# Transposing normalised tokens and attention output by DMA, with the settings of the order of work chosen anew

## Chip, cores and metric

The kernel runs on one core of one Trainium2 chip. The metric is the time of one execution on the device in microseconds (us). A core has five engines with lists of instructions of their own: TensorE (PE, with its weight loads PEld), VectorE (DVE), ScalarE (ACT), GpSimd (POOL) and SyncE (SP), which here issues all DMAs.

## The reference

Two layers of attention and feed-forward on 2048 tokens of width 512, in bfloat16; attention has 32 heads of 16 channels, the feed-forward part 1792 channels. Both layers use the same weights.

```
def _A_ref(x, wqkv, wo):                        # H = 32, Dh = 16
    q, k, v = split((x @ wqkv).reshape(B, S, 3, H, Dh))
    p = softmax(einsum("bhqd,bhkd->bhqk", q, k) * Dh ** -0.5)
    return einsum("bhqk,bhkd->bhqd", p, v).reshape(B, S, D) @ wo
def _B_ref(x, w_gate, w_up, w_down):
    return (gelu(x @ w_gate) * (x @ w_up)) @ w_down
x = A_x
x = x + _A_ref(_layernorm(x), A_wqkv, A_wo)
x = x + _B_ref(_layernorm(x), B_w_gate, B_w_up, B_w_down)
x = x + _A_ref(_layernorm(x), A_wqkv, A_wo)
x = x + _B_ref(_layernorm(x), B_w_gate, B_w_up, B_w_down)
```

## The kernel before

**Attention.** Tokens are cut into blocks of queries: four of 512 in layer 0, three of 512 and two of 256 in layer 1, the last of these split into two halves of 128 for its last two groups. A *unit* is one block and one group of four heads. Each unit passes twice over the scores. In pass 1 TensorE makes score tiles of 128 queries x 512 keys (line 2236) into PSUM banks 0 to 3, and DVE takes the maximum of each row (`p1_emit`, line 2251), for two banks in one instruction where two are free (128x1024), else for one (128x512). A *folded* tile is another way to these maxima: TensorE makes the score difference of two key blocks (KD, line 2059), ACT rectifies it (line 2066), and one DVE instruction (line 2246) adds it to the score tile of one block and takes the maximum, so that one pass does for two tiles. `fin_step` and `negmax` bring the maxima of a unit into its query tile by four small DMAs (line 1416). In pass 2 TensorE makes the transposed scores with the maximum taken off (line 2114), ACT takes the exponential (line 2086, one or two banks), and TensorE multiplies with the values into bank 7 (line 2139). `nrm` divides and writes ATT.

**The rest.** It is written as chains (Python generators), each of which says which engine it wants next, what it reads and writes, and when it is due. `outproj` takes a finished block: for each 128 tokens it transposes ATT into ATTT (two buffers), multiplies with WO and adds to X. `ln_to_xnt` normalises tiles of X into XN (two buffers; by `ln_pool` on GpSimd alone, `ln_head`, or `ln_fast` at the very end), and each XN tile is transposed into XNT. `ffn` does gate, up and down products from XNT; `kproj`, `vproj` and `qproj` make keys, values and queries from XNT. Both transposes go through `transpose_tile`: four TensorE transposes of 128x128 into one borrowed bank, then `evac`, a copy out of the bank by ACT or DVE (lines 1110 and 1108). Which of the two does an eviction is decided by the lead of pass 1 over pass 2.

**The order.** No engine decides at run time: a planner in `_build` simulates all engines while it writes their lists. Its clock gives every instruction a duration; for DMAs, SyncE is taken for 0.63 us an issue, and the data has landed 1.6 us plus a term after that:

```
            if grp is not None:
                clk[eng] = start + T_DMA * nd
                done = max(clk["dma"], clk[eng] + 1.6) + dur
                clk["dma"] = done - 1.6
```

At each step the planner looks which score tiles, exponentials and chain steps could start now and takes one by rules. A dummy product (line 2269) fills TensorE where it would idle long. Twenty numbers steer the rules: among them LAG (the lead of pass 1 over pass 2, in pairs of tiles, from which pass 2 may use banks 3 to 6, the *wide* mode), LAGT and LAGX (the lead from which evictions go to DVE), FL (how small the lead must be for folding) and PIECE (how much of a chain's product goes in one piece). `PLAN` gives new values at numbered stretches of pass 1, each of two tile pairs. The wait between instructions follows from what each reads and writes (`_Sched`), and each engine does its list strictly in order.

The first stretch of the time, in which the input is normalised, is the *head*; the one between the layers, where keys and values of layer 1 must be made before its second pass can start, is the *seam* (about 1200 to 1350 us).

Of the kernel before, what the change touches and what calls it, by code (L numbers as in the profile page):

```python
# [608 lines left out]
def _build(nc, x_in, wqkv, wo, wg, wu, wd, out, layer_blocks=((512, 512, 512, 512), (512, 512, 512, 256, 256)),  # L609
# [16 lines left out]
    with es:  # L626
# [137 lines left out]
        def bank(b):  # L764
            return PS[:, b, :]
# [1734 lines left out]
```

## Time and profile before

| | |
|---|---|
| median of 3 runs | 2471.88 us (2471.85 to 2478.18) |
| the profiled execution's own time | 2472.17 us |
| its span, first to last instruction | 2470.4 us |
| mean granted TensorE clock | 1.000 |
| DVE busy | 2405.3 us (97%) |
| ACT busy | 2342.4 us (95%) |
| POOL busy | 1318.4 us (53%) |
| DMA, mean | 10 GB/s |

The profile lists one execution. In its groups, `out<-in (partitions x elements, type) xcount | busy us, mean ns | idle before, and what ended it`. ACT's and DVE's instructions overlap a little at their ends, so the busy time of a group can be less than count times mean. Bank tiles are called PS, the exponentials and folded tiles SCR. Line numbers such as L2251 are those of the kernel before.

### The profile page before, as it was taken

What the parts mean: (1) busy time and instruction counts of PE and PEld (TensorE: products, weight loads), DVE (VectorE), ACT (ScalarE), POOL (GpSimd) and SP (SyncE); (2) the same over time, 40 slices, a digit from 0 to 9 for tenths busy, and PEclk for the clock granted to TensorE, in tenths of its full rate; (3) what the DMA queues carried; (4) which work ended last, traced back from release to release, by engine and by line L of the source; (5) the groups of instructions that cost most, each with busy time, mean ns of one, the idle gap of its engine ahead of it and who ended that gap; (6) DMA issues with size and microseconds to landing.
All of it is one profiled execution on the core that took longest, in us unless ns stands there. A gap on an engine that the chain in (4) does not pass through costs nothing.

```text
span 2470.4 us, 69276 instructions
## 1 busy us (share of the span) xinstructions
PE 2407.1 (97%) x29766; PEld 1145.6 (46%) x29766; DVE 2405.3 (97%) x3167; ACT 2342.4 (95%) x3252; POOL 1318.4 (53%) x2181
## 2 busy tenths in 40 slices
PE   8999999999999999999999999999999999999999
PEld 3454444444444444444433555554444444544456
DVE  9999999999999999999999999999999999999995
ACT  7999999999999999999976999999999999999997
POOL 5121148965779367957143211279517882379472
PEclk9999999999999999999999999999999999999999
DMA  3110000000000000000000000000000000000000
GB/s 97 47 57 8 4 4 6 2 4 4 4 4 2 4 5 4 4 6 6 10 13 14 5 4 4 4 4 2 6 8 7 2 2 9 6 5 3 10 5 11
DMA packets 27388, 25.13 MB, mean 10 GB/s; under 512 B 9544, under 2 KB 26056, under 8 KB 27080
## 3 DMA queue, kind: packets, MB, share of 16 engines
q1 hardware_dynamic: 27080, 20.69, 3.0%
q8 instruction: 233, 3.82, 0.7%
q14 instruction: 75, 0.61, 0.1%
HBM read 9.70 MB, written 2.10 MB: 5 GB/s over the span
## 4 chain that ended last, share of the span: by engine, by line
DVE 39%; PE 38%; ACT 22%; issue 1%; POOL 1%; POOLq 0%; ACTq 0%; DVEq 0%
DVE PM L2251 37%; ACT SCR L2086 20%; PE PS L2236 13%; PE PS L1093 10%; PE PS L2139 9%; PE PS L2114 4%; PE PS L2269 2%; DVE SCR L2246 1%; DVE HT L891 0%; PE PS L2059 0%; ACT SCR L2066 0%; ACT SCR L1588 0%; PE PS L1222 0%; ACT AO L1760 0%; ACT ACCS L1440 0%
## 5 line engine op out<-in xcount | busy, mean ns | idle before, releaser
L2251 DVE TENSOR_REDUCE PM<-PS 128x1 f32<-128x512 f32 (+1 forms) x2581 | 2234.2, 931 | 29.1 <-PE PS L2236 8.3
L2086 ACT ACTIVATE SCR<-PS 128x1024 bf16<-128x1024 f32 (+1 forms) x2529 | 2028.5, 897 | 54.4 <-PE PS L2114 37.8
L2236 PE MATMUL PS<-KT,QT 32*128 32x512 bf16 x3938 | 1037.8, 385 | 36.6 <-DVE PM L2251 20.5
L2114 PE MATMUL PS<-QT,KT 32*128 32x512 bf16 (+2 forms) x4864 | 953.4, 349 | 6.4 <-ACT SCR L2086 4.7
L2139 PE MATMUL PS<-VP,SCR 128*128 128x51 bf16 (+1 forms) x16384 | 818.0, 187 | 9.4 <-ACT SCR L2086 4.9
L2139 PEld LDWEIGHTS PS<-VP,SCR 128*128 128x128 bf16 x16384 | 576.0, 96 | 507.3 <-issue 433.1
L2236 PEld LDWEIGHTS PS<-KT,QT 32*128 32x128 bf16 x3938 | 247.7, 91 | 509.5 <-DVE PM L2251 306.1
L1446 POOL TENSOR_TENSOR RL<-ACCS,CM 128x16 f32<-128x16 f32 (+2 forms) x66 | 179.5, 2720 | 382.5 <-ACT ACCS L1440 382.2
L2269 PE MATMUL PS<-WV,ZER 128*128 128x240 bf16 x1866 | 350.7, 265 | 0.7 <-ACT SCR L2086 0.6
L2114 PEld LDWEIGHTS PS<-QT,KT 32*128 32x128 bf16 x4864 | 241.6, 91 | 73.1 <-ACT SCR L2086 43.7
L1387 POOL TENSOR_TENSOR PM<-PM 128x32 f32<-128x32 f32 (+2 forms) x76 | 18.3, 241 | 312.9 <-DVE PM L2251 300.6
L1762 POOL TENSOR_TENSOR HT<-HT,AO 128x512 bf16<-128x512 bf16 (+1 forms) x107 | 119.6, 1121 | 84.5 <-ACT AO L1760 83.5
L2269 PEld LDWEIGHTS PS<-WV,ZER 128*128 128x128 bf16 x1866 | 142.4, 96 | 46.6 <-issue 37.7
L1093 PE MATMUL PS<-XNT,WG 128*128 128x512 bf16 (+2 forms) x560 | 139.4, 339 | 0.3 <-ACT HT L1110 0.2
L1093 PE MATMUL PS<-XNT,WU 128*128 128x512 bf16 (+2 forms) x560 | 137.9, 339 | 0.9 <-ACT AO L1760 0.7
L1093 PE MATMUL PS<-WD,HT 128*128 128x512 bf16 x448 | 134.7, 381 | 0.0
L1822 POOL TENSOR_TENSOR KD<-KT 128x512 bf16<-128x512 bf16 x74 | 85.3, 1153 | 70.7 <-PE PS L2059 68.5
L1582 POOL TENSOR_TENSOR SCR<-HT 128x512 bf16<-128x512 bf16 (+1 forms) x98 | 95.9, 979 | 29.0 <-ACT HT L1110 13.9
L1592 POOL TENSOR_TENSOR HT<-HT,SCR 128x512 bf16<-128x512 bf16 (+1 forms) x98 | 106.0, 1083 | 3.8
L1586 POOL TENSOR_TENSOR SCR<-SCR,HT 128x512 bf16<-128x512 bf16 (+1 forms) x98 | 106.0, 1083 | 1.9
L2246 DVE CUSTOM_DVE_ANT_0 SCR<-PS,SCR 128x512 bf16<-128x512 f32 x158 | 101.3, 685 | 1.4 <-PE PS L2059 0.6
L1466 POOL TENSOR_TENSOR X<-X,AO 128x512 f32<-128x512 f32 x42 | 53.2, 1268 | 79.5 <-ACT AO L1464 79.1
(129 smaller groups left out, 1558.3 us busy)
## 6 DMA issues: line engine op xcount, KB each, us to landing
KT<-SG SPq DMA_DIRECT2D x64, 64.0 KB
QT<-SG SPq DMA_DIRECT2D x56, 64.0 KB
QT<-MT SPq DMA_DIRECT2D x216, 1.0 KB
out_dram<-AO SPq DMA_DIRECT2D x16, 128.0 KB, 1.7
WG<-in_B_w_gate_dram SPq DMA_DIRECT2D x4, 448.0 KB, 4.1
WU<-in_B_w_up_dram SPq DMA_DIRECT2D x4, 448.0 KB, 4.9
WD<-in_B_w_down_dram SPq DMA_DIRECT2D x4, 384.0 KB, 4.5
QT<-MT SPq DMA_DIRECT2D x72, 0.5 KB
```

The source lines that it names most:

```text
L1093: ins = e.matmul(out_ap, lhsT=l, rhs=r_, start=(i == 0), stop=(i == n - 1))
L1446: emit("pool", lambda e: e.tensor_tensor(RL[:, s, 0:4 * nq], lsum, CM1[:, 0:4 * nq], op=ALU.pow), r=[("ACCS", s), ("CM1",)], w=[("RL", s)] ...
L1586: emit("pool", lambda e: e.tensor_tensor(u, u, ht, op=ALU.mult), r=ku + kh, w=ku, dur=0.18 + n / 520.0)
L1592: emit("pool", lambda e: e.tensor_tensor(ht, ht, u, op=ALU.mult), r=ku + kh, w=kh, dur=0.18 + n / 520.0)
L1762: emit("pool", lambda e, ft=ft, o=o: e.tensor_tensor(HV[:, ft, :], HV[:, ft, :], AO[:, o, 0:n], op=ALU.mult), r=[("AO", o)] + ht_keys(ft, ...
L2086: emit("act", lambda e: e.activation(dst, src, ACTF.Exp, scale=DH ** -0.5), r=[BK[bk + i] for i in range(cnt)], w=[("PT", i) for i in slot ...
L2114: ins = e.matmul(bank(bk)[:, i * n:(i + 1) * n], lhsT=KT[32 * j:32 * j + 32, g, kt * 128:(kt + 1) * 128], rhs=QT[32 * j:32 * j + 32, s, c0 ...
L2139: ins = e.matmul(acc, lhsT=PT[:, slot, i * nh + (qt - q0) * 128:i * nh + (qt - q0 + 1) * 128], rhs=AP(VP, (kt * H + 4 * g + j) * 17, [[NTT ...
L2236: ins = e.matmul(bank(b), lhsT=QT[32 * j:32 * j + 32, s, qt * 128:(qt + 1) * 128], rhs=KT[32 * j:32 * j + 32, g, kb * 512:(kb + 1) * 512], ...
L2246: emit("dve", lambda e, i=i, b=b, sl=sl: e.tensor_tensor_reduce(PT[:, sl, :], bank(b), PT[:, sl, :], 1.0, -3.0e38, ALU.add, ALU.max, po[:, ...
L2251: emit("dve", lambda e: e.tensor_reduce(po, PS[:, bs[0]:bs[0] + cnt, :], axis=AX.X, op=ALU.max), r=bks, w=[("PM", sm) + h[1:] for h in hs] ...
L2269: return e.matmul(PS[:, b, NACC:512], lhsT=ZER[:, :], rhs=WV[:, 0, 0:512 - NACC], start=(b != 7), stop=(b != 7), skip_group_check=True)
```

## The change

38 tiles of normalised tokens and 27 tiles of attention output are transposed by DMA from SBUF to SBUF, issued by SyncE, four DMAs of 128x128 to a tile, in place of four TensorE transposes and an eviction. Transposes at the head, at the seam (the last 512 tokens of layer 0 before its feed-forward, their attention output, and the last 512 tokens at the input of layer 1) and those before the feed-forward part of the last 256 tokens stay on TensorE, and so does the attention output of the last 128 tokens. The DMA of a tile has a group of its own for each of the two buffers, so that each landing can be waited for alone. `PLAN` is replaced as a whole: 426 entries become 573, from the same kinds of values. A bank is named as written in `ln_fast` where X3 is on, and the output of a split last tile uses groups of its own where TH is on; X3 and TH are 0.

```
 PLAN = {
-    0: (0.1, 0.15, 0.45, 0.42, 0.3, -0.05, 3, 1, 62, 84, 8, 60, 0.0, 2.0, 0, 2, 2, 2, 7, 84),
...
+    0: (0.4, 0.35, 0.65, 0.32, 1.0, -0.05, 3, 1, 62, 84, 8, 100, 0.1, 1.5, 10, 10, 1, 4, 11, 84),
...
-           ... LAGX=84, G2=0, CAL=0):
+           ... LAGX=84, G2=0, CAL=0, XD=3, XDT=0.6):
...
-        out_groups = ["st_out0", "st_out1"]
+        out_groups = ["st_out0", "st_out1"] + (["st_out2", "st_out3"] if TH else [])
...
+        if XD:
+            move_groups += ["xt0", "xt1", "at0", "at1"]
...
+        def transpose_dma(src_fn, rkeys, dst_fn, wkeys, grp):
+            emit("sp", lambda e: [e.dma_start_transpose(out=dst_fn(ck), in_=src_fn(ck)) for ck in range(NCK)],
+                 r=list(rkeys), w=list(wkeys), grp=grp, nd=NCK, dur=XDT)
+
         def ln_to_xnt(tts, tag, ready, due, fast=False):
...
                 yield ("cond", lambda i=i: at["xn"] >= i)
+                if XD & 1 and not fast and (tts[-1] < 12 or (tag[0] == "mid" and tag[1] == NL - 1)):
+                    yield ("sp", [("XN", i % 2)], [("XNT", tt)])
+                    transpose_dma(lambda ck, i=i: XN[:, i % 2, ck * 128:(ck + 1) * 128], [("XN", i % 2)],
+                                  lambda ck, tt=tt: XNT[:, ck, tt * 128:(tt + 1) * 128], [("XNT", tt)], "xt%d" % (i % 2))
+                    xnt_rec[tt] = tag
+                    at["tr"] = i
+                    continue
                 yield ("pe", [("XN", i % 2)], [("XNT", tt)])
...
+            dt = XD & 2 and not lastb and (la == NL - 1 or t0 + n < S)
+
             def tr(qt):
+                if dt:
+                    transpose_dma(lambda ck: ATT[:, a0 + qt, ck * 128:(ck + 1) * 128], ak,
+                                  lambda ck: ATTT[:, qt % 2, ck, :], [("ATTT", qt % 2)], "at%d" % (qt % 2))
+                    if qt == nq - 1:
+                        att_free["bi"] = bi
+                    return
                 transpose_tile(lambda ck: ATT[:, a0 + qt, ck * 128:(ck + 1) * 128], ak, ATTT[:, qt % 2, :, :],
                                [("ATTT", qt % 2)])
...
-            yield ("pe", ak, [("ATTT", 0)])
+            yield ("sp" if dt else "pe", ak, [("ATTT", 0)])
```

More of the change, by code (lines that the diff above doesn't have):

```diff
@@ L609, in _build @@
 def _build(nc, x_in, wqkv, wo, wg, wu, wd, out, layer_blocks=((512, 512, 512, 512), (512, 512, 512, 256, 256)),
-           n_ahead=6, n_pre=6, S1C=0.45, S2C=0.42, OV=0.3, PD=80, FDUE=20, LIM=-0.05, NT=1, AHD=2.0, DUEM=2, FDL2=0, OPD=12, URG=0.3, ft_tok=512, n_pt=8, n_qt=8, SPLIT=0.15, SPC=0.1, PVC=47, WARM=0.55, WARML=0.42, NPV=7, BOOST=0.0, LAG=62, LAGT=84, GP=2, SING=0, DUE=0, END=360, LAGE=10, FD=205, FDL=-10, QD=60, KD_=16, VD=20, FL=8, FMAX=6, NKD=2, FLOOK=2, FX=0.3, GF=0, FAST=1, TG=1, GS=2, P2B=1, PIECE=2, GL=60, GLE=20, HARD=-1e9, LNP=1, LNPT=12, PREO=1, SPL=2, OPL=1, BM=1, LAGB=60, PREO0=1, LNPT0=8, LNPT1=8, QH0=2, QH1=2, OPS=12, FDS=0, FD3=205, FDA=0, SPL0=0, VCH=0, TA=0, TC=0, X3=0, TH=0, HQ=0, TP=1, LAGX=84, G2=0, CAL=0):
+           n_ahead=6, n_pre=6, S1C=0.45, S2C=0.42, OV=0.3, PD=80, FDUE=20, LIM=-0.05, NT=1, AHD=2.0, DUEM=2, FDL2=0, OPD=12, URG=0.3, ft_tok=512, n_pt=8, n_qt=8, SPLIT=0.15, SPC=0.1, PVC=47, WARM=0.55, WARML=0.42, NPV=7, BOOST=0.0, LAG=62, LAGT=84, GP=2, SING=0, DUE=0, END=360, LAGE=10, FD=205, FDL=-10, QD=60, KD_=16, VD=20, FL=8, FMAX=6, NKD=2, FLOOK=2, FX=0.3, GF=0, FAST=1, TG=1, GS=2, P2B=1, PIECE=2, GL=60, GLE=20, HARD=-1e9, LNP=1, LNPT=12, PREO=1, SPL=2, OPL=1, BM=1, LAGB=60, PREO0=1, LNPT0=8, LNPT1=8, QH0=2, QH1=2, OPS=12, FDS=0, FD3=205, FDA=0, SPL0=0, VCH=0, TA=0, TC=0, X3=0, TH=0, HQ=0, TP=1, LAGX=84, G2=0, CAL=0, XD=3, XDT=0.6):
     S = x_in.shape[1]
@@ L1134, in ln_fast @@
                 if pb is not None:
-                    emit("act", lambda e, tt=tt: e.activation(X[:, tt, :], bank(pb), ACTF.Copy), r=[BK[pb]], w=[("X", tt)], dur=0.482)
+                    emit("act", lambda e, tt=tt: e.activation(X[:, tt, :], bank(pb), ACTF.Copy), r=[BK[pb]], w=[("X", tt), BK[pb]], dur=0.482)
                     held.discard(pb)
@@ L1548, in outproj @@
                 if qt + 1 < nq:
-                    yield ("pe", ak, [("ATTT", 1 - s)])
+                    yield ("sp" if dt else "pe", ak, [("ATTT", 1 - s)])
                     tr(qt + 1)
@@ L1785, in ffn @@
                                                                           OB[o][:, c * hw:(c + 1) * hw]),
-                             r=[("OB", o, c)], grp=out_groups[c], dur=0.5)
+                             r=[("OB", o, c)], grp=out_groups[2 + c], dur=0.5)
                     ffn_rec[tt] = la
```

987 rows, old and new, of the table PLAN are left out of this document.

## The prediction

> **What bounds the kernel now.** I read the page first, for the shares of the engines and the chain that ended last, then the busy times by stretch, to see where which engine has room, and last the groups of instructions kept apart by shape, for prices.
>
> ```profile
> span 2470.4 us, 69276 instructions
> PE 2407.1 (97%) x29766; PEld 1145.6 (46%) x29766; DVE 2405.3 (97%) x3167; ACT 2342.4 (95%) x3252; POOL 1318.4 (53%) x2181
> DVE 39%; PE 38%; ACT 22%; issue 1%; POOL 1%; POOLq 0%; ACTq 0%; DVEq 0%
> ...
> L2269 PE MATMUL PS<-WV,ZER 128*128 128x240 bf16 x1866 | 350.7, 265 | 0.7 <-ACT SCR L2086 0.6
> ```
> ```profile
> 60.00:350.00 290.00, 284.01 (x3705) 140.43 (x3704) 287.28 (x416) 286.03 (x340) 51.48 (x97) 1.00 0.08 25
> 350.00:1200.00 850.00, 826.72 (x10078) 381.92 (x10077) 844.74 (x1016) 828.74 (x1201) 599.35 (x993) 1.00 0.02 4
> 1200.00:1350.00 150.00, 146.16 (x1041) 53.75 (x1038) 143.27 (x247) 103.95 (x142) 54.51 (x103) 1.00 0.05 14
> 1350.00:1600.00 250.00, 244.46 (x3531) 128.48 (x3526) 247.21 (x310) 249.71 (x278) 50.75 (x85) 1.00 0.02 4
> 1600.00:2350.00 750.00, 737.35 (x9355) 348.02 (x9352) 738.16 (x920) 729.25 (x1051) 464.24 (x694) 1.00 0.02 5
> 2350.00:2470.40 120.40, 115.68 (x1726) 70.21 (x1725) 89.15 (x147) 100.43 (x181) 64.09 (x138) 1.00 0.03 8
> ```
>
> Each row gives a stretch, its length, and busy time with count for PE, PEld, DVE, ACT and POOL, then the granted clock. VectorE (DVE) and ScalarE (ACT) carry the kernel together. From 350 to 1200 us, where the feed-forward work of layer 0 runs beside attention, DVE is busy 844.74 of 850 and ACT 828.74. TensorE's 97% misleads: 350.7 us of it are the dummy products of line 2269. So a saving counts if it takes time from DVE, or from ACT where ACT's time can be turned into DVE's.
>
> It can. The maxima of the scores are taken on DVE by line 2251; "folding" lets ACT write a rectified difference of two score tiles, and one DVE pass then does the work of two.
>
> ```profile
> L2251 DVE TENSOR_REDUCE PM<-PS 128x2 f32<-128x1024 f32 x1199 | 1452.2, 1218 | 18.9 <-PE PS L2236 6.0 <-PE PS L2114 4.2 <-PE PS L2059 0.3
> L2251 DVE TENSOR_REDUCE PM<-PS 128x1 f32<-128x512 f32 x1382 | 926.9, 682 | 10.1 <-PE PS L2114 4.0 <-PE PS L2236 2.3
> L2246 DVE CUSTOM_DVE_ANT_0 SCR<-PS,SCR 128x512 bf16<-128x512 f32 x158 | 101.3, 685 | 1.4 <-PE PS L2059 0.6 <-PE PS L2236 0.4
> L2246 DVE DVE_READ_ACCUMULATOR2_ANT PM<- 128x1 f32 x158 | 13.2, 83 | 0.0
> L2066 ACT ACTIVATE SCR<-PS 128x1024 bf16<-128x1024 f32 x76 | 79.5, 1046 | 11.8 <-PE PS L2059 11.4
> ```
>
> Four score tiles cost DVE two pair reductions of 1452.2/1199 = 1.21 us, 2.42 together. Folded they cost 2 x (101.3+13.2)/158 = 1.45, and ACT one 1.05. A fold so buys 0.97 of DVE for 1.05 of ACT. The order written by the planner folds whenever ACT has caught up with DVE, so freed ACT time can flow over by itself.
>
> **What the change removes.** By the conditions in the diff, 38 normalised tiles (12 and 14 before the feed-forward of the two layers, 12 at the input of layer 1) and 27 attention tiles (12 and 15) lose four TensorE transposes and one eviction each. The seam (1200 to 1350) and the head keep theirs. The evictions of the two stretches and the one of the last 256 tokens that goes:
>
> ```profile
> L1110 ACT ACTIVATE XNT<-PS 128x512 bf16<-128x512 bf16 x23 | 14.2, 618 | 0.0
> L1110 ACT ACTIVATE ATTT<-PS 128x512 bf16<-128x512 bf16 x12 | 8.0, 662 | 0.0
> L1108 DVE COPY XNT<-PS 128x512 bf16<-128x512 bf16 x1 | 0.4, 416 | 0.0
> ...
> L1110 ACT ACTIVATE ATTT<-PS 128x512 bf16<-128x512 bf16 x10 | 6.2, 623 | 0.1
> L1110 ACT ACTIVATE XNT<-PS 128x512 bf16<-128x512 bf16 x9 | 5.8, 649 | 0.1
> L1108 DVE COPY XNT<-PS 128x512 bf16<-128x512 bf16 x5 | 2.1, 415 | 0.0
> L1108 DVE COPY ATTT<-PS 128x512 bf16<-128x512 bf16 x4 | 1.7, 415 | 0.0
> ...
> 2441.28 0.40 DVE L1108 COPY ATTT<-PS 128x512 bf16<-128x512 bf16 x1
> ```
>
> Counted: 23+12+9+10 = 54 on ACT and 1+5+4+1 = 11 on DVE, the 65 tiles. ACT loses 14.2+8.0+6.2+5.8 = 34.2 us, DVE 0.4+2.1+1.7+0.4 = 4.6 us. If none of ACT's time is turned over, the span loses DVE's 4.6. If it is turned over until both gain alike, k folds with 34.2 - 1.05k = 4.6 + 0.97k give k = 14.7 and 18.8 us on each. I take 12, the middle: in the stretch from 350 to 1200 ACT already leaves 21 us idle beside a full DVE, so not each freed microsecond will be used, but a backlog of ACT is what keeps folds out there.
>
> TensorE loses 260 transposes. That I cost at nothing on the path, since the dummy products leave it room; but the bank that a transpose borrows puts the score tiles to single banks meanwhile. Two single reductions cost 2 x 926.9/1382 = 1.34 against 1.21 for a pair, 0.13 more; 65 tiles that each cost one split would be 8 us. I count none of it and keep it as the low end.
>
> **What it adds.** 260 transposing DMAs, four to a tile, issued by SyncE. No row shows such a DMA; the nearest are plain ones.
>
> ```profile
> 1759.50 2.21 SPq L1416 DMA_DIRECT2D QT<-MT  x4
> 1797.44 2.27 SPq L1416 DMA_DIRECT2D QT<-MT  x4
> ...
> out_dram<-AO SPq DMA_DIRECT2D x16, 128.0 KB, 1.7
> WG<-in_B_w_gate_dram SPq DMA_DIRECT2D x4, 448.0 KB, 4.1
> WU<-in_B_w_up_dram SPq DMA_DIRECT2D x4, 448.0 KB, 4.9
> ...
> SPq L1416 <- DVE MT L1398: 1174.1, 56, 40.3
> ```
>
> Four issues take 2.21 us, so SyncE gets about 65 x 2.21 = 144 us more, and it waits 1174.1 us for line 1398 alone: room enough. Moved past: the four issues that bring the maxima into the queries (line 1416) can stand 2.2 us behind a tile's transposes; the settings let the maxima lead the exponentials by tens of tile pairs (the mean stands below), so that is covered, and uncovered it would cost 2.2 us at that unit.
>
> The planner reserves 4 x 0.63 + 1.6 + 0.6 = 4.72 us from the first issue to the landing. If a transpose lands like the 128 KB store, the tile is there at 2.21 - 0.55 + 1.7 = 3.4 us, sooner than reserved, and nobody waits. If it lands like the WU load, it is 2.21 - 0.55 + 4.9 = 6.6, or 1.8 late. I take the store's side, 3.4 to 4.7, since a transpose moves 32 KB between two tiles on the core, where the load reads a tensor in DRAM.
>
> Latency under the reserve is hidden. Tiles normalised on GpSimd follow each other slowly, and the two buffers of XN cover 4.7 us:
>
> ```profile
> 367.10 0.77 POOL L1212 TENSOR_SCALAR XN<-X,LNS 128x512 bf16<-128x512 f32 x1
> 382.17 0.77 POOL L1212 TENSOR_SCALAR XN<-X,LNS 128x512 bf16<-128x512 f32 x1
> ...
> 961.61 0.77 POOL L1157 TENSOR_SCALAR XN<-X,LNS 128x512 bf16<-128x512 f32 x1
> 963.84 0.77 POOL L1157 TENSOR_SCALAR XN<-X,LNS 128x512 bf16<-128x512 f32 x1
> ...
> 2433.68 0.29 POOL L1451 TENSOR_TENSOR ATT<-ACCS,RL 128x64 bf16<-128x64 f32 x1
> 2439.99 0.38 PE L1222 MATMUL PS<-IDN,ATT 128*128 128x128 bf16 x4
> ```
>
> The first pair stands 15 us apart. The second, from the quicker normalisation of line 1157, stands 2.2 apart and will be held back some 2 us a tile; its block has a unit of attention as cover (1797.44 - 1759.50 = 38 us above), except for tiles 12 and 13 near the end, where up to 4 us could show. At the very end the attention tile is ready at 2433.97 and its transpose starts only at 2439.99, behind other TensorE work; a DMA of 4.7 us lands at 2438.7. So the one tile of the last 256 that the condition lets through costs nothing and may gain 1 us. The other two edits (a bank named as written, output groups 2 and 3) sit in branches whose switches are 0: nothing.
>
> The settings cannot be priced row by row. Weighted by stretch, the mean lead that opens the wide mode falls from 46 to 40, and the one that sends evictions to DVE from 92 to 82. The unit is the 0.13 us of a split pair: 60 pairs more or fewer make 8 us either way. I take 0.
>
> Sum: 12 us off the profiled execution's 2472.17 us (0.3 above the median of 2471.88): **2460 us**.
>
> [...]
>
> **Rivals.** *Late landing (slower).* TensorE takes its list in order, so a product that comes up before its transposed tile has landed blocks the score products queued behind it, and DVE and ACT run dry. 27 attention products and 7 feed-forward blocks are such places. At the 1.8 us late of the WU load, 34 x 1.8 = 61 us of stall; filled banks hide about one reduction of 1.2 us only now and then, so I count half: 2460 + 31 = 2491. It decides where 34 half-delays eat the 12, at 0.7 us late. For it: no transposing DMA was seen. Against: the store's 1.7. Its chance is 0.18.
>
> *No turnover (same).* DVE stays full, ACT idles more: 2472 - 4.6 = 2467.6. For it: 21 us of ACT lie unused from 350 to 1200. Chance 0.17.
>
> *The new settings cost (slower).* More splitting of pairs: 170 further splits at 0.13 are 22 us, 2460 + 22 = 2482. Over 149 decide it. For it: the lower lead opens the wide mode, which serves single banks, more often. Chance 0.08.
>
> **How the numbers follow.** The main case has the remaining 0.57, at 2460, and on its own 2445 (18.8 and 8 from fewer splits) to 2464. About 0.3% (7.4 us) is what a measurement of this kernel can tell from no change: the main case lies beyond it, no turnover within it, the other two beyond it on the slow side. So faster 0.57, same 0.17, slower 0.26. The range 2444 to 2491 leaves out the longer half of the late landings and a little below.
>
> **What would show it.** Right: evictions to XNT and ATTT are 65 fewer; line 2246 rises by some 20 to 30 passes; DVE's busy time is about 12 us lower; TensorE shows no new waits for DMA. Wrong: products reading ATTT wait for a DMA in the waits (late landing); ACT's idle time grows by 30 with the passes of line 2246 unchanged (no turnover); the single-bank count of line 2251 well above 1382 (settings).

## The result: 2.9% slower, and the profile after

The kernel after takes 2545.43 us (median of 4 runs, 2538.06 to 2555.83) against 2471.9 before: ratio 1.0294, 95% interval 1.0253 to 1.0335. The forecast of 2460 and its range to 2491 were wrong. The profile is of the execution of 2538.06 us. Its page (span, busy times, granted clock in 40 slices, and the chain that ended last by engine and by line) reads:

```profile
span 2536.3 us, 69328 instructions
PE 2429.0 (96%) x29685; PEld 1149.3 (45%) x29685; DVE 2399.4 (95%) x3253; ACT 2325.2 (92%) x3104; POOL 1267.6 (50%) x2167
PEclk9999989999999998999999999999999999989989
PE 34%; DVE 32%; ACT 22%; SPq 5%; POOL 3%; DMA 2%; issue 2%; POOLq 0%; ACTq 0%; DVEq 0%
```

DVE is busy for 2399.4 us, 5.9 less than before, yet the span is 65.9 longer: DVE's idle time went from 65.1 to 136.9 us. The chain names a new member, SyncE's queue (SPq) with 5%, and DMA with 2%. The busy times by stretch show where (columns as in the prediction):

```profile
60.00:350.00 290.00, 281.12 (x3691) 139.63 (x3689) 287.44 (x422) 285.34 (x339) 50.72 (x103) 1.00 0.09 26
350.00:1200.00 850.00, 814.12 (x9696) 369.20 (x9694) 816.08 (x1064) 798.79 (x1100) 568.13 (x981) 0.98 0.05 11
1600.00:2350.00 750.00, 715.63 (x8976) 337.18 (x8972) 704.12 (x888) 697.10 (x939) 429.20 (x658) 0.97 0.04 9
```

The first stretch, almost without the new DMAs, is as full as before. From 350 to 1200 DVE falls from 844.74 to 816.08, from 1600 to 2350 from 738.16 to 704.12, and the granted clock from 1.00 to 0.98 and 0.97. The line that issues the new DMAs (duration of one issue as min/median/max in ns; then who waited, in us and times; then the time from an issue to its landing):

```profile
L1378 SPq DMA_TRANSPOSE XNT<-XN x152: 1093/1232/2401, 380.2 to 2410.1; - x152
L1378 SPq DMA_TRANSPOSE ATTT<-ATT x108: 1093/1232/2614, 344.7 to 2504.1; - x108
...
  PE PS L1242: 35.2, 18
...
DMA to landing us min/median/max: 2.2/2.3/4.6
```

One issue holds SyncE's queue for 1.23 us. Four take 4.9, against 2.21 for the four plain ones that the prediction priced by. The largest of the waits, read in the chain of the trace from 982 to 996 us (start, duration, what), shows the mechanism:

```profile
981.97 1.17 SPq L1378
...
989.55 1.23 SPq L1378
990.78 0.04 issue
990.83 2.34 DMA XNT<-XN
993.17 0.14 issue
993.31 0.59 PE PS L1242
```

Eight issues stand one behind the other (two tiles), then the last one lands 2.34 us after its start, and only then the feed-forward product on line 1242 starts. Ahead of the eight stand four query issues of line 1576 (from 979.65), and ahead of those eight more for two other tiles (from 968.73), so the queue had no pause since then. TensorE stood still for 5.69 us and DVE for 6.09 behind it. TensorE's timeline after that stop, and the busy times of those 10 us and the next:

```profile
993.31 0.59 PE L1242 MATMUL PS<-XNT,WG 128*128 128x512 bf16 x1 [5.69 <-DMA XNT<-XN]
993.99 0.61 PE L2404 MATMUL PS<-KT,QT 32*128 32x512 bf16 x2
...
997.21 0.61 PE L1242 MATMUL PS<-XNT,WG 128*128 128x512 bf16 x1
...
997.92 0.40 PE L2404 MATMUL PS<-KT,QT 32*128 32x512 bf16 x1
```
```profile
990.00:1000.00 10.00, 6.69 (x58) 2.64 (x59) 4.34 (x6) 4.27 (x7) 1.38 (x2) 0.66 0.04 7
1000.00:1010.00 10.00, 9.96 (x111) 4.24 (x109) 9.63 (x12) 9.86 (x16) 9.04 (x11) 1.00 0.01 2
```

For some four microseconds after the stop the same products take 0.6 us instead of 0.4, and the granted clock of those 10 us is 0.66; in finer stretches it is 0.50 from 993.3 to 997.2 and 1.00 from 998 on. So this late tile cost its wait of 5.69 us and then slow products on top. A longer stop did not bring a longer half clock here, as the first late tile of all and the stretch behind it show:

```profile
356.75 1.01 PE L1242 MATMUL PS<-WO,ATTT 128*128 128x512 bf16 x2 [2.12 <-DMA ATTT<-ATT]
```
```profile
360.00:370.00 10.00, 10.00 (x76) 3.66 (x74) 6.74 (x7) 6.88 (x12) 6.39 (x11) 0.50 0.12 25
```

After a wait of 2.12 us the clock stayed at 0.50 for about 13 us; in the ten of the row TensorE was busy all the time and DVE two thirds of it. After a wait of 2.01 us for another attention tile, which ended at 660.97, it stayed at 1.00.

### The profile page after: what moved, and what is told of

It reads as the page before. It is cut to its first block, busy times and chain, and to the rows that moved or that the text cites. A ratio compares the mean times of both kernels' runs of the same rounds, so it can differ in the third digit from the quotient of the medians.

```text
span 2536.3 us, 69328 instructions
## 1 busy us (share of the span) xinstructions
PE 2429.0 (96%) x29685; PEld 1149.3 (45%) x29685; DVE 2399.4 (95%) x3253; ACT 2325.2 (92%) x3104; POOL 1267.6 (50%) x2167
## 4 chain that ended last, share of the span: by engine, by line
PE 34%; DVE 32%; ACT 22%; SPq 5%; POOL 3%; DMA 2%; issue 2%; POOLq 0%; ACTq 0%; DVEq 0%
DVE PM L2419 28%; ACT SCR L2254 20%; PE PS L2404 11%; PE PS L1242 10%; PE PS L2307 7%; SPq L1378 5%; PE PS L2282 3%; PE PS L2437 2%; DVE SCR L2414 2%; POOL RL L1606 1%; ACT SCR L2234 1%; DMA ATTT<-ATT 1%; DVE HT L1922 1%; POOL XN L1322 1%; DMA XNT<-XN 1%
## 5 line engine op out<-in xcount | busy, mean ns | idle before, releaser
L2419 DVE TENSOR_REDUCE PM<-PS 128x1 f32<-128x512 f32 (+1 forms) x2506 | 2167.9, 925 | 97.1 <-PE PS L2282 62.6
L2254 ACT ACTIVATE SCR<-PS 128x1024 bf16<-128x1024 f32 (+1 forms) x2442 | 2015.4, 927 | 122.9 <-PE PS L2282 102.7
L2282 PE MATMUL PS<-QT,KT 32*128 32x512 bf16 (+2 forms) x4864 | 928.6, 353 | 4.4 <-DMA QT<-MT 2.2
L2437 PE MATMUL PS<-WV,ZER 128*128 128x240 bf16 x2045 | 383.6, 267 | 1.3 <-ACT SCR L2254 1.2
L2282 PEld LDWEIGHTS PS<-QT,KT 32*128 32x128 bf16 x4864 | 234.1, 91 | 71.7 <-ACT SCR L2254 40.7
L2437 PEld LDWEIGHTS PS<-WV,ZER 128*128 128x128 bf16 x2045 | 155.2, 96 | 54.8 <-issue 45.7
L2414 DVE CUSTOM_DVE_ANT_0 SCR<-PS,SCR 128x512 bf16<-128x512 f32 x224 | 144.2, 684 | 3.6 <-PE PS L2282 1.7
L2234 ACT ACTIVATE SCR<-PS 128x1024 bf16<-128x1024 f32 (+1 forms) x115 | 119.4, 1043 | 12.1 <-PE PS L2227 11.1
```

Source lines behind the costliest of these rows:

```text
L2234: emit("act", lambda e: e.activation(PT[:, s0:s0 + cnt, :], PS[:, bk:bk + cnt, :], ACTF.Relu), r=bks, w=[("PT", s0 + d) for d in range(cnt ...
L2254: emit("act", lambda e: e.activation(dst, src, ACTF.Exp, scale=DH ** -0.5), r=[BK[bk + i] for i in range(cnt)], w=[("PT", i) for i in slot ...
L2282: ins = e.matmul(bank(bk)[:, i * n:(i + 1) * n], lhsT=KT[32 * j:32 * j + 32, g, kt * 128:(kt + 1) * 128], rhs=QT[32 * j:32 * j + 32, s, c0 ...
L2414: emit("dve", lambda e, i=i, b=b, sl=sl: e.tensor_tensor_reduce(PT[:, sl, :], bank(b), PT[:, sl, :], 1.0, -3.0e38, ALU.add, ALU.max, po[:, ...
L2419: emit("dve", lambda e: e.tensor_reduce(po, PS[:, bs[0]:bs[0] + cnt, :], axis=AX.X, op=ALU.max), r=bks, w=[("PM", sm) + h[1:] for h in hs] ...
L2437: return e.matmul(PS[:, b, NACC:512], lhsT=ZER[:, :], rhs=WV[:, 0, 0:512 - NACC], start=(b != 7), stop=(b != 7), skip_group_check=True)
```

## The experiments

Two theories were open at first. A: the price of issuing. B: the order and its settings are slower in themselves. Later came C and T, two ways in which the DMAs but not their time on the queue would be to blame. In all kernels below except e7 and e8 the order of instructions on every engine is that of the kernel after; only what SyncE issues for a tile differs. Ratios are to the kernel before.

**Plain copies in the same places (e1).** The tiles are moved, but stay untransposed; so do those that are copied plainly in e2 and e3.

```
- e.dma_start_transpose(out=dst_fn(ck), in_=src_fn(ck))
+ e.dma_start(dst_fn(ck), src_fn(ck))
```

> Every engine has the list of the changed kernel, instruction for instruction; only each of the 260 transposing DMAs is a plain copy of the same 128 x 128 elements, so that XNT and ATTT hold those tiles untransposed. Theory A (price of the issue): a transposing DMA holds SyncE for 1.23 us (median of 260 in the changed kernel) where the planner reserves 0.63 and a plain one takes 0.55; a tile's four take 4.9 in place of 2.5 and land after about 6, later still in a burst, and TensorE blocks on them. Then with plain copies a tile lands within 4.72 us, the waits of TensorE for XNT and ATTT (39 us) are gone, the granted clock is 1.00 again, and the time is 2455 to 2475. Theory B (the order by the new settings is itself the slower one): it stays at 2530 or more with DVE still idle for over 120 us.

2469.64 us, ratio 0.9993 (0.9984 to 1.0002). The line of the new DMAs in e1:

```profile
L1378 SPq DMA_DIRECT2D XNT<-XN x152: 464/601/1827, 375.0 to 2347.9; - x152
...
DMA to landing us min/median/max: 1.7/1.8/3.7
```

0.60 us an issue, no wait of TensorE for such a tile, and the 76 us are gone. Order and settings are not what costs: B falls.

**One kind of tile alone (e2, e3).** e2 keeps the 152 transposing DMAs of the normalised tiles and copies the attention tiles plainly; e3 the other way round.

```
+ e.dma_start_transpose(...) if grp[0] == "x" else e.dma_start(...)    # e2; "a" in e3
```

> As the kernel with plain copies, but the 152 DMAs of the normalised tiles transpose again; the 108 of the attention tiles stay plain copies, so ATTT holds them untransposed. Theory A: the waits for ATTT (22 us in the changed kernel) are gone, those for XNT (17 us) remain or shrink, since the queue ahead of them is shorter; by these shares of the loss the time is 32 us over the plain one, about 2490 to 2505. Theory B: no different from the changed kernel, 2535 to 2555.

> The other half: the 108 DMAs of the attention tiles transpose, the 152 of the normalised tiles are plain copies, so XNT holds those untransposed. Theory A: the waits for ATTT remain near 20 us, those for XNT go, and the time is about 40 us over the plain one, 2495 to 2515; if the losses of the two halves simply add, this kernel and its sibling make up the whole loss. Theory B: 2535 to 2555.

e2: 2503.82 us, ratio 1.0123 (1.0105 to 1.014). e3: 2519.49, ratio 1.019 (1.0174 to 1.0205). Above e1 that is 34.2 and 49.9 us, together 84, where the kernel after lies 75.8 above e1, so the two losses nearly add. e3 is 4.5 us above the range of A, and far below that of B. TensorE's waits for such tiles (waiter, releaser: us in total, times, longest), first of e2, then of e3:

```profile
PE PS L1242 <- DMA XNT<-XN: 15.9, 5, 8.3
PE PS L2307 <- DMA XNT<-XN: 6.5, 1, 6.5
```
```profile
PE PS L1242 <- DMA ATTT<-ATT: 14.8, 7, 3.7
PE PS L2282 <- DMA ATTT<-ATT: 2.4, 1, 2.4
PE PS L2404 <- DMA ATTT<-ATT: 0.7, 1, 0.7
```

The waits alone make 22.4 and 17.9 us, less than what is lost. In e2 they grew, where A had them remain or shrink (17.1 for XNT in the kernel after).

**One DMA for a whole tile (e4).** A tile of 128x512 is transposed by one DMA into its four blocks. The planner still reserves the time of four, so that the order stays.

```
- emit("sp", lambda e: [e.dma_start_transpose(out=dst_fn(ck), in_=src_fn(ck)) for ck in range(NCK)], ..., nd=NCK)
+ emit("sp", lambda e: e.dma_start_transpose(out=dst_fn(slice(0, NCK)), in_=src_fn(slice(0, NCK))), ..., nd=1, cn=NCK)
- clk[eng] = start + T_DMA * nd
+ clk[eng] = start + T_DMA * (cn or nd)
```

> The order of the changed kernel on every engine, but each tile of 128 x 512 is transposed by one DMA in place of four; the result is the reference's. If SyncE's 1.23 us are a price for each DMA, a tile takes 1.23, lands after some 3.6 us, under the 4.72 reserved, and theory A expects 2450 to 2475. If they are a price for the elements moved, a tile still takes 4.9 and the time stays at 2535 to 2555. In between, as a fixed part of about 0.5 and a part for the elements, a tile takes 3.4 and lands near 4.5 to 5: 2460 to 2490. Theory B: 2530 or more in every case.

2468.85 us, ratio 0.9989 (0.998 to 0.9998). The line of the DMAs and the busy times of e4:

```profile
L1378 SPq DMA_TRANSPOSE XNT<-XN x38: 1188/1192/2270, 373.3 to 2342.7; - x38
...
DMA to landing us min/median/max: 2.3/2.4/4.2
```
```profile
PE 2365.0 (96%) x29445; PEld 1142.1 (46%) x29685; DVE 2395.4 (97%) x3253; ACT 2320.7 (94%) x3104; POOL 1269.4 (51%) x2167
```

The issue of four times the data takes 1.19 us, it lands after 2.4, and nobody waits for it. The same tiles are transposed by DMA at the same places of the order, without the loss. What costs is not that a DMA transposes them, but that four such issues do it.

**Two and three DMAs to a tile (e5, e6).** Is each further issue dear, or only those past what the order reserves?

```
+ cuts = [(0, 2), (2, 4)]            # e5;  [(0, 2), (2, 3), (3, 4)] in e6
+ emit("sp", lambda e: [e.dma_start_transpose(out=dst_fn(slice(a, b)), in_=src_fn(slice(a, b))) for a, b in cuts], ...)
```

> The kernel after, each tile transposed by two DMAs of 128x256 instead of four of 128x128; the order of every engine stays. Theory A (the price is the time that SyncE takes for an issue, about 1.23 us of any width, and it hurts only where the last landing passes the 4.72 us that the order reserves): two issues 2.4 us, the last landing about 1.2 + 2.4 = 3.6 us after the start, inside the reserve, so the time of the one-issue kernel, 2469 us, within 4. Rival C (each transposing DMA beyond the first costs its share, reserve or not): a third of the 76 us, about 2494.

> The kernel after, each tile transposed by three DMAs (128x256, 128x128, 128x128); the order stays. Theory A: three issues take 3.7 us where 2.5 are reserved, the last landing at about 2 x 1.23 + 2.4 = 4.9 us, at the edge of the 4.72 reserved; a tile alone is hardly late, tiles close behind each other are by 1.2 us each: 2470 to 2490. Rival C (linear in the number of DMAs): 2469 + 76 x 2/3 = 2520.

e5: 2469.49 us, ratio 0.9988 (0.9979 to 0.9998). e6: 2492.62, ratio 1.0091 (1.0066 to 1.0117). Two cost nothing, three 24 us, 2.6 us above what A allowed: C is out. In e6 TensorE waits again:

```profile
L1379 SPq DMA_TRANSPOSE XNT<-XN x114: 1191/1233/2297, 374.8 to 2366.2; - x114
...
  PE PS L1242: 4.5, 5
```

**As much queue time without any transposing (e9, e10).** Eight plain copies of 128x64 to a tile, or six (four of them 128x64, two 128x128).

```
+ cuts = [(0, 64), (64, 128), ..., (448, 512)]
+ emit("sp", lambda e: [e.dma_start(dst_fn(a, b), src_fn(a, b)) for a, b in cuts], ...)
```

> The kernel after, each tile moved by eight plain copies of 128x64 in place of the four transposing DMAs (so the tiles stay untransposed); the order of every engine stays. Theory A (only the time counts that the issues of a tile keep SyncE's queue busy, whatever they do): 8 x 0.60 = 4.8 us per tile, as the four transposing DMAs with 4 x 1.23 = 4.9, so 2530 to 2555. Rival T (it is the transposing itself, its descriptors or the way through the transposer, that makes the tiles late): at most the 2470 of four plain copies, and 2480 at the outside.

> The kernel after, each tile moved by six plain copies (four of 128x64, two of 128x128), untransposed; the order stays. Theory A: 6 x 0.60 = 3.6 us per tile, as three transposing DMAs with 3.7: 2480 to 2500. Rival T: 2470.

e9: 2557.74 us, ratio 1.0348 (1.0318 to 1.0377). e10: 2499.17, ratio 1.0098 (1.0078 to 1.0117). The line of e9:

```profile
L1379 SPq DMA_DIRECT2D XNT<-XN x304: 464/601/1848, 383.3 to 2438.1; - x152
...
  PE PS L1242: 42.0, 19
```

Plain copies do the same harm, if they hold the queue for as long. T is out, though e9 lies 2.7 us above A's range. Nor is it the count of issues: six plain ones (e10) cost about as much as three transposing ones (e6). All kernels with this order side by side, by the median duration of an issue:

| issues to a tile | queue held, us | time, us |
|---|---|---|
| 1 transposing, 128x512 (e4) | 1.2 | 2468.85 |
| 4 plain (e1) | 4 x 0.60 = 2.4 | 2469.64 |
| 2 transposing, 128x256 (e5) | 2 x 1.25 = 2.5 | 2469.49 |
| 6 plain (e10) | 6 x 0.60 = 3.6 | 2499.17 |
| 3 transposing (e6) | 3 x 1.23 = 3.7 | 2492.62 |
| 8 plain (e9) | 8 x 0.60 = 4.8 | 2557.74 |
| 4 transposing (after) | 4 x 1.23 = 4.9 | 2545.43 |

The planner reserves 4 x 0.63 = 2.5 us of the queue for a tile. Up to there the time is flat; past it, it climbs steeply, by 24 to 30 us for the first 1.2 us and by another 53 to 59 for the next. What the DMAs do hardly matters. The last landing moves along with the queue time: from the gaps and landings measured (0.64 us from one plain issue to the next, 1.27 from one transposing issue to the next, 1.8 and 2.3 to 2.4 to land) it comes at an estimated 3.7 us after the first start in e1 and e5, 4.8 in e6, 5.0 in e10, 6.1 in the kernel after and 6.3 in e9, against the 4.72 reserved. These runs cannot tell which of the two reserves decides, the 2.5 us of queue or the 4.72 to the landing. The order of the last four by landing is that of their times; but the runs of e9 (2549.5 to 2566.23) overlap those of the kernel after, and those of e10 those of e6.

**Settings and order apart (e7, e8).** e7 has the new settings and leaves all transposes on TensorE; e8 has the settings of before and e4's one DMA to a tile. Here the order changes.

```
- XD=3, XDT=0.6      + XD=0, XDT=0.6       # e7
- PLAN = {new}       + PLAN = {before}     # e8, on top of e4
```

> The new settings with all transposes left on TensorE, as in the kernel before. Theory S1 (the settings are an improvement, or at least neutral, in themselves): about 2460 to 2480. Theory S2 (the settings are fitted to the one order in which the transposes are DMAs, and put on another program they decide wrongly at each later step): over 2500.

> The settings of the kernel before, with the transposes as one DMA per tile in the places of the change. Theory S1 (the moved transposes bring their gain under any settings): 2460 to 2472. Theory S2 (settings fit one program only): over 2490, so that the freed 34 us of ScalarE can't be read from this run at all.

e7: 2600.9 us, ratio 1.0522 (1.0504 to 1.0539). e8: 2538.13, ratio 1.0268 (1.0252 to 1.0283). S1, by which settings or moved transposes bring their gain on their own, is out. Neither has tiles that land late; their busy times, e7's and then e8's:

```profile
PE 2483.2 (96%) x30003; PEld 1194.2 (46%) x30254; DVE 2434.1 (94%) x3287; ACT 2354.1 (91%) x3209; POOL 1291.2 (50%) x2170
```
```profile
PE 2423.7 (96%) x29569; PEld 1160.8 (46%) x29831; DVE 2412.9 (95%) x3167; ACT 2334.1 (92%) x3189; POOL 1308.0 (52%) x2174
```

DVE and ACT have more work or more idle time than before (DVE idles 163.7 and 123.8 us, against 65.1). The settings decide at numbered steps of one program; on the two programs that they were not chosen for, the time is 129 and 66 us above the kernel before. So these runs cannot price the moved transposes apart from their settings, and what both are worth together shows in e1, e4 and e5: 2 to 3 us, with intervals that come close to no change or, in e1, include it.

## Why the prediction was wrong, point by point

**The step that failed** is the price of the added DMAs: "Four issues take 2.21 us, so SyncE gets about 65 x 2.21 = 144 us more". It took the row of a small plain copy for a transposing DMA. The size was no fault (a plain copy of a whole 128x128 block costs about the same, 0.60 in e1), the kind was. Measured: 1.23 us an issue, 260 x 1.23 = 320 us. From this the landing follows: with the gaps of 0.04 between issues seen in the chain, the last of four lands 3 x 1.27 + 2.3 = 6.1 us after the first starts, 1.4 past the 4.72 reserved, and twice the 0.7 at which the prediction itself saw its sign turn. The landing of one DMA, 2.3 us, was not the fault; it lies nearer to the store's 1.7 than to the load's 4.9.

**"Latency under the reserve is hidden"** looked at the normalised tiles, which come singly or in pairs. The attention tiles come four together, and their sixteen issues run into one another. SyncE's queue in the kernel after, from 944 us, and the same sixteen, as plain copies, in e1:

```profile
944.79 21.20 SPq L1378 DMA_TRANSPOSE ATTT<-ATT  x16
...
968.73 10.88 SPq L1378 DMA_TRANSPOSE XNT<-XN  x8
```
```profile
933.65 14.42 SPq L1378 DMA_DIRECT2D ATTT<-ATT  x16
```

In the kernel after the 16 issues held the queue for 21.2 us without a pause. In e1 they were through in 14.4, and between the second tile and the third the queue stood free for 4.4 of them. A price that is wrong by 0.6 us an issue so uses up the pause and still becomes a delay of some seven microseconds. The query issues (line 1576) that were "covered" stayed so: TensorE's score products of line 2282 waited 2.2 us for them in all. But they did their part the other way round: in the largest wait they stand ahead of the tiles.

**The first rival, late landing, is what happened,** with the place that it named (products on line 1242 that read ATTT and XNT), but at 31 us where 76.6 were measured (2545.43 less e4's 2468.85). It expected 61 us of waits at 34 places and halved them, because filled banks would hide some. Measured: TensorE stood still 18 times and 35.2 us in all (the 3.9 us of its weight loads for such tiles fall into the same stops), and more than twice as much was lost. So little can have been hidden, and the rival had no term for the slow products after a stop.

They make most of the rest: over stretches of 1 us the granted clock of the kernel after is at one half for some 89 us, 80 of them busy (e4's mean granted clock is 1.00, that of the kernel after 0.983). A product of 512 columns follows the one before it after 0.54 us there and 0.32 otherwise (the chain, from 994 and from 998 us), so of those 80 us an estimated 33 are lost. With the waits that makes 68; the profiled execution, 2538.06 us, is 69 above e4. The same sum for the other kernels with late tiles comes within 4 us of what their profiled executions lost against e4 (e6) or e1 (e2, e3, e9, e10): 42 + 50 of 93 in e9, 18 + 35 of 53 in e3. This is an account from traces; no run held the clock up with the waits left in.

**The gain: 12 us forecast, 3 measured** where nothing lands late (e4). The evictions went as counted: to XNT and ATTT there are 24 + 3 on ACT and 2 + 2 on DVE left of 82 and 14, 65 fewer. The turnover came, in another form. From the groups of DVE by shape in e4:

```profile
L2419 DVE TENSOR_REDUCE PM<-PS 128x2 f32<-128x1024 f32 x1142 | 1385.7, 1216 | 23.9 <-PE PS L2282 9.4 <-PE PS L2404 6.9 <-PE PS L2227 0.7
L2419 DVE TENSOR_REDUCE PM<-PS 128x1 f32<-128x512 f32 x1364 | 914.6, 680 | 12.7 <-PE PS L2282 5.7 <-PE PS L2404 3.1 <-PE PS L2227 0.3
L2414 DVE CUSTOM_DVE_ANT_0 SCR<-PS,SCR 128x512 bf16<-128x512 f32 x224 | 144.1, 684 | 2.5 <-PE PS L2282 0.7 <-PE PS L2404 0.6 <-PE PS L2227 0.3
L1922 DVE TENSOR_TENSOR HT<-PS,HT 128x512 bf16<-128x512 f32 x48 | 32.6, 679 | 0.2 <-PE PS L1242 0.2
L2414 DVE DVE_READ_ACCUMULATOR2_ANT PM<- 128x1 f32 x224 | 18.5, 83 | 0.0
```

The passes of the fold rose by 66 (158 to 224, 33 pairs), more than twice the 20 to 30 named as a sign. DVE's score work fell from 2493.6 to 2462.9 us, by 30.7: 33 pairs at the 0.93 us that this makes each, close to the 0.97 of the prediction. But the new order gave DVE 48 up-products of 128x512 (line 1922, 32.6 us; none before), which ACT and GpSimd shared until now; the prediction had no term for such a shift. With 4.2 us of these evictions less, some 4 us of others into HT and small items, DVE's busy time came out 9.9 us lower, near the 12, but by luck: the 30.7 less and the 32.6 more cancel. The term left out is the wait: DVE's idle time rose by 6.5 us (65.1 to 71.6), all of it before the reductions of line 2419 (23.9 + 12.7 us, against the 18.9 + 10.1 that the prediction's rows show before them). A busy time saved is not a span saved; here two thirds went into waits, which those rows put down mostly to score products (lines 2282 and 2404). Why the order found no better use of it is open.

**The settings at 0** had no ground. The unit chosen (split pairs) did not move against the kernel: single reductions went from 1382 to 1364. But these runs can't price settings and program apart (e7, e8). The last tile of the last 256 tokens cost nothing, as forecast, where issues were cheap: in e4 nobody waited for it.

**A transposing DMA beside a plain one.** With 128x128 to an issue the transposing DMA took 1.23 us (kernel after) against 0.60 for a plain copy of the same tile (e1), and 2.3 us to the landing against 1.8. With 128x512 to an issue a tile takes 1.19 us (e4), where four plain copies take 2.4; one plain copy of 128x512 was in no run.

## What to carry to other kernels

Price a DMA by the time that its issue holds the queue and the landing that follows from it, and look for a row of the same kind of DMA; where there is none, the prediction's range must reach at least to twice the nearest row, the factor here (1.23 us against 0.55 to 0.60), since the fixed reserves of this plan let an excess of 0.6 us an issue become a delay of some seven. Where a DMA's issue costs the same at every width measured (here 1.19 to 1.25 us for 128, 256 and 512 columns), cut the number of DMAs, not the bytes: one for the whole tile made the loss of 76 us vanish. Do not price a stop of TensorE at its length alone: here the slow products behind the stops cost an estimated 33 us on top of 35. And an order fitted step by step to one program is part of that program: compare changes under it only with the order held still.

## What the hardware showed that was not expected

- The issue of a transposing DMA took 1.19 to 1.25 us on SyncE for 128x128, 128x256 and 128x512 alike, and landed 2.3 to 2.4 us after its start; the plain copy of 128x128 took 0.60 and landed after 1.8, that of 128x64 the same.
- A stop of TensorE of 5.7 us was followed by about four microseconds in which products took 0.6 instead of 0.4 us; a stop of 2.1 us by about 13 us at a granted clock of 0.50, and one of 2.0 us by none.
- Busy times hide this loss: in the kernel after TensorE shows 96% and DVE 95%. The chain that ended last, with SPq at 5%, and the granted clock of single 10 us stretches showed it.
